# A fused attention and feed-forward kernel: single PSUM banks for the plain chunks, tile waits for new pools, and other places for the wide chunks' attention

## The chip, the core and the metric

The kernel runs on one core of a Trainium2 chip. The metric is the device time of one execution in microseconds (us). The engines are named as in the profile: PE is the matrix engine (TensorE), DVE VectorE, ACT ScalarE, POOL GpSimd, and SP the engine from whose queue nearly all transfers (DMA) are issued. PEld is PE's loading of weights.

## The reference

Inputs are `q`, `k`, `v` of shape 8 x 8 x 576 x 64 (batch, heads, sequence, head dimension), a gain `g_norm` of 64, and two weight matrices of 512 x 2048 and 2048 x 512. All is float32.

```python
kv = np.einsum('bhsd,bhse->bhde', k, v)
out = np.einsum('bhsd,bhde->bhse', q, kv)
rms = np.sqrt(np.mean(out * out, axis=-1, keepdims=True) + 1e-06)
x = (out / rms * g_norm)            # then heads are laid side by side: 4608 x 512
h = x @ w_in
g = 0.5 * h * (1.0 + erf(h / np.sqrt(2.0)))
result = g @ w_out
```

So there is a linear attention without softmax (a 64 x 64 matrix per head, then a product with the queries), a root-mean-square norm per head and token, and a two-layer network with an exact GELU.

## The kernel before

The 4608 tokens are cut into seven chunks: two **plain** chunks of 512 tokens (0 and 1) and five **wide** ones of 704, 704, 736, 736 and 704 tokens (2 to 6). Every float32 operand of a matmul is split into a rounded high part and the low rest; a product is the sum of high x high, low x high and high x low, three matmuls.

**Plain chunks** take 16 steps each. A step computes one block of 128 hidden units: `layer1` (line 621, twelve matmuls at L636 into one bank called h), `gelu` on ACT, which writes the high part `gh` and the whole value back into the bank (lines 649, 650), `rest` on DVE, which makes the low part `gl` (line 660), and `second_layer` (L668, twelve matmuls into four accumulator banks). Layer 2 of a step comes on PE behind layer 1 of the step after. Beside it run the conversion of the weights, sums of weight blocks that are stored to DRAM as `products`, and the attention of the next chunk.

**Wide chunks** (class `Fast`, lines 1096 to 1236) use a Strassen-Winograd scheme: seven products of half-size blocks in place of eight. Layer 1 has 28 steps (u = 0 to 27; group m = u // 7 and product k from `ORDER`), twelve matmuls each at L1127; layer 2 has 28 more (u = 28 to 55, list `TICKS`), at L1208. Each step reads one 512 KB block of `products` from DRAM, through a ring of six tiles (`fetch`, `used`, L547). In layer 1 the products go to pairs of banks X, Y and Z by turns, and DVE adds earlier results to them (`behind`, L564) before ACT applies GELU; the next product on the same pair waits for that. `ready` (L1186) splits an operand of layer 2: high part on ACT (L1195), low part on DVE (L1196). `combine` (L1184) adds blocks, partly on POOL.

The attention of chunk c + 1 runs inside chunk c (function `within`, line 1251) at steps that a table of numbers gives: loads of keys and queries, the key sum (`sum_keys`, L194, one pair of batches), four projections (L395) into pair W with their squares (L422, L423, L430), `fold` and `rsqrt` (the root: four small ACT copies, then nine small passes on DVE, lines 315 to 335), four `scale` (a spreading transpose on DVE, L346, into the single buffer `sq`, then a multiply on POOL, L342), four `add_blocks` (POOL, L448), and the seven `piece` splits (L456, L457). For chunk 2, called `FAST` in the table, all of this stood late (`LATE_...`: sum at step 18, projections at 20 to 26, root at 29, scales at 30 to 33, which is layer 2).

**Banks and pools.** PSUM is eight banks; before, they are four tiles of two banks each, X, Y, Z and W, for the whole kernel. A plain chunk's bank h0 or h1 is one half of X, its a0 or a1 half of W, its accumulators the halves of Y and Z. In SBUF a pool `top` gives way to `first_room` at step 13 of chunk 1 and a pool `low` to `last_room` at step 6 of chunk 2; the tiles named d are in these two rooms.

The order on each engine is the order of the program text (`manual_schedule`); a tile waits for the instructions that used it or its place before.

## Time and profile before

| what | value |
| --- | --- |
| three runs | 807.11, 813.13, 818.93 us; median 813.13 us |
| profiled execution | 813.25 us, of which the span of the profile is 811.5 us |
| PE busy | 758.6 us, 93% |
| PEld busy | 704.6 us, 87% |
| DVE busy | 540.7 us, 67% |
| ACT busy | 356.4 us, 44% |
| POOL busy | 173.8 us, 21% |
| DMA | 233.66 MB, mean 288 GB/s |

Busy shares are means over stages with different limits. The plain chunks run until 224.74 us, then come the five wide ones. The views read below are PE's waits (who released it after it stood idle), tables of busy time for stretches of the span, and the instructions of one engine in order of time; in those a number in brackets behind a row is the idle time before it, with what ended it.

### The profile page before, as it was taken

Reading aid. Unit: us, or ns where it says so; the run is one execution under the profiler, and the core shown is the slowest. Engines: PE = TensorE matmul, PEld = TensorE weight load, DVE = VectorE, ACT = ScalarE, POOL = GpSimd, SP = SyncE. Lnnn points to the kernel's source line nnn. Section 1 sums busy time; section 2 is a strip of 40 time slices with the busy share of each in tenths; the row PEclk is TensorE's granted clock in tenths of the full one; section 3 lists DMA queues with packets and bytes.
Section 4 is the critical chain, followed back from the end, with each engine's and each line's share of the span. In section 5 each row is a group of like instructions: output and inputs, shape, how many; then the busy total and the mean of one; then the engine's idle time right before and its main releaser. Section 6 shows DMA issues by size and latency. Waiting matters only on the chain.

```text
span 811.5 us, 13272 instructions
## 1 busy us (share of the span) xinstructions
PE 758.6 (93%) x5150; PEld 704.6 (87%) x5150; DVE 540.7 (67%) x720; ACT 356.4 (44%) x554; POOL 173.8 (21%) x127
## 2 busy tenths in 40 slices
PE   7799989997898996999898999899999899999997
PEld 6687777886798995999898999889998899999997
DVE  2899969989453468944659924579634679543782
ACT  3688735543352362604435415426325346123550
POOL 1000046333152107001262001380002370012000
PEclk9999999999998999999999999999999999999999
DMA  9995982794689975899688998788997788998895
GB/s 348 407 360 168 370 302 104 263 328 162 229 270 370 350 249 175 264 372 371 222 259 263 331 410 301 226 276 266 329 408 269 239 255 291 316 317 295 294 311 178
DMA packets 84962, 233.66 MB, mean 288 GB/s; under 512 B 8484, under 2 KB 29476, under 8 KB 84900
## 3 DMA queue, kind: packets, MB, share of 16 engines
q1 hardware_dynamic: 84896, 232.82, 82.0%
q8 instruction: 41, 0.67, 0.3%
q14 instruction: 21, 0.17, 0.1%
q10 hardware_dynamic: 4, 0.00, 0.0%
HBM read 193.99 MB, written 38.80 MB: 287 GB/s over the span
## 4 chain that ended last, share of the span: by engine, by line
PE 59%; DVE 21%; DMA 9%; issue 5%; ACT 4%; SPq 1%; POOL 1%; DVEq 0%; ACTq 0%
PE banks_Z L1127 8%; PE banks_Z L1208 7%; PE banks_Y L1127 7%; PE banks_X L1127 7%; PE banks_X L636 7%; PE banks_Y L1208 6%; DVE d L1196 5%; PE banks_X L1208 4%; DMA w_in<-products_in 4%; DVE d L1184 3%; PE banks_Y L668 2%; DMA w_in<-products_out 2%; DMA d<-kv_main 2%; PE banks_Z L668 2%; PE banks_W L194 2%
## 5 line engine op out<-in xcount | busy, mean ns | idle before, releaser
L1196 DVE TENSOR_TENSOR d<-d,d 128x704 fp32r<-128x704 f32 (+1 forms) x140 | 127.8, 936 | 59.4 <-ACT d L1195 59.3
L1195 ACT CAST d<-d 128x704 fp32r<-128x704 f32 (+1 forms) x140 | 104.4, 786 | 42.5 <-DVE d L1184 38.7
L1208 PE MATMUL banks_Z<-d,w_in 128*128 128x352 f32 (+1 forms) x720 | 116.8, 320 | 6.5 <-DVE d L1196 5.9
L1127 PE MATMUL banks_Z<-d,w_in 128*128 128x352 f32 (+1 forms) x684 | 116.4, 321 | 4.7 <-DVE e L564 4.7
L1208 PEld LDWEIGHTS banks_Z<-d,w_in 128*128 128x128 f32 x720 | 111.6, 191 | 9.4 <-DVE d L1196 8.6
L1127 PEld LDWEIGHTS banks_Z<-d,w_in 128*128 128x128 f32 x684 | 107.1, 191 | 7.3 <-DVE e L564 6.1
L636 PE MATMUL banks_X<-x,w_in 128*128 128x512 f32 x360 | 85.8, 389 | 13.5 <-DVE gl L660 13.5
L636 PEld LDWEIGHTS banks_X<-x,w_in 128*128 128x128 f32 x360 | 67.8, 192 | 28.5 <-DVE gl L660 18.5
L1127 PE MATMUL banks_Y<-d,w_in 128*128 128x352 f32 (+1 forms) x480 | 83.0, 324 | 6.7 <-DVE e L564 6.1
L564 DVE TENSOR_TENSOR e<-banks_Z,e 128x704 f32<-128x704 f32 (+1 forms) x53 | 47.7, 900 | 58.9 <-PE banks_Z L1127 50.6
L1184 POOL TENSOR_TENSOR d<-d,d 128x704 f32<-128x704 f32 (+1 forms) x15 | 25.7, 1715 | 283.6 <-ACT d L1139 283.6
L1127 PEld LDWEIGHTS banks_Y<-d,w_in 128*128 128x128 f32 x480 | 75.7, 193 | 10.7 <-DVE e L564 6.9
L1208 PE MATMUL banks_X<-d,w_in 128*128 128x352 f32 (+1 forms) x480 | 77.3, 318 | 6.6 <-DVE d L1196 6.6
L1127 PE MATMUL banks_X<-d,w_in 128*128 128x352 f32 (+1 forms) x480 | 81.1, 319 | 0.9 <-DMA w_in<-products_in 0.9
L1208 PEld LDWEIGHTS banks_X<-d,w_in 128*128 128x128 f32 x480 | 74.2, 191 | 7.6 <-DVE d L1196 7.6
L1127 PEld LDWEIGHTS banks_X<-d,w_in 128*128 128x128 f32 x480 | 75.1, 191 | 3.0 <-issue 2.7
L1208 PE MATMUL banks_Y<-d,w_in 128*128 128x352 f32 (+1 forms) x480 | 75.7, 316 | 1.3 <-DMA w_in<-products_out 0.7
L1208 PEld LDWEIGHTS banks_Y<-d,w_in 128*128 128x128 f32 x480 | 73.2, 189 | 2.6 <-issue 1.4
L564 DVE TENSOR_TENSOR e<-banks_Y,e 128x704 f32<-128x704 f32 (+2 forms) x31 | 27.3, 880 | 44.0 <-PE banks_Y L1208 35.2
L1184 DVE TENSOR_TENSOR d<-d,d 128x704 f32<-128x704 f32 (+1 forms) x45 | 51.0, 1133 | 0.0
L649 ACT ACTIVATE gh<-banks_X 128x512 fp32r<-128x512 f32 x32 | 19.1, 597 | 69.5 <-PE banks_X L636 64.2
L1139 ACT ACTIVATE d<-e 128x704 f32<-128x704 f32 (+1 forms) x20 | 16.0, 801 | 66.4 <-DVE e L564 66.4
(179 smaller groups left out, 1034.5 us busy)
## 6 DMA issues: line engine op xcount, KB each, us to landing
w_in<-products_in SPq DMA_DIRECT2D x140, 512.0 KB, 4.9
w_in<-products_out SPq DMA_DIRECT2D x140, 512.0 KB, 4.5
products_in<-w_in SPq DMA_DIRECT2D x40, 256.0 KB, 4.9
w_in<-w_in SPq DMA_DIRECT2D x16, 512.0 KB, 10.2
w_out<-w_out SPq DMA_DIRECT2D x16, 512.0 KB, 10.2
products_out<-w_out SPq DMA_DIRECT2D x32, 256.0 KB, 5.0
...
```

The costliest lines, as they stand in the source:

```text
L194: nc.tensor.matmul(out=ps[r, n * D:(n + 1) * D], lhsT=k[:, r], rhs=v[:, r], start=(j == 0), stop=(j == NJ),)
L564: return eng.tensor_tensor(out=out, in0=x, in1=y, op=op)
L636: nc.tensor.matmul(out=h, lhsT=parts["in", i][:, w][:, p * P:(p + 1) * P], rhs=woven(at.x[p][:, x]), start=(m + p == 0), stop=(m == 2 and ...
L649: nc.scalar.activation(out=to, in_=h, func=AF.Gelu)
L668: nc.tensor.matmul(out=ps, lhsT=x[:, ts], rhs=woven(parts["out", i][:, w]), start=(i == 0 and m == 0), stop=(m == 2 and i == NF - 1),)
L1127: nc.tensor.matmul(out=ps[:, n], lhsT=y, rhs=woven(x[:, z, kb]), start=k in (0, 2, 1) and kb + i == 0, stop=kb == 1 and i == 2, skip_group ...
L1139: nc.scalar.activation(out=self.grid(self.blocks[m][side][1])[:, half], in_=src, func=AF.Gelu)
L1184: eng.tensor_tensor(out=out, in0=x, in1=y, op=op)
L1195: nc.scalar.copy(out=t[:, 0], in_=src)
L1196: nc.vector.tensor_tensor(out=t[:, 1], in0=src, in1=t[:, 0].bitcast(F32), op=ALU.subtract)
L1208: nc.tensor.matmul(out=ps[:, a], lhsT=y, rhs=woven(x[:, z, p]), start=k in (0, 2, 1) and n + p + i == 0, stop=n == GROUPS - 1 and p == 1 a ...
```

## The change

Five things change together.

1. **Banks.** The plain chunks' banks are tiles of one bank each (h0, h1, a0, a1 and four accumulators), in two pools. The pairs X and W are made anew from the one pool before chunk 2, the pairs Y and Z from the other behind the plain chunks' last store. The projections of chunk 2 use a0 and a1, and their squares are taken in halves.
2. **Waits.** The pools `first_room`, `last_room` and the two new PSUM pools are made with `reuse_waits="tile"`: a tile waits for the users of the memory that it covers itself.
3. **Tables.** In chunk 2 the attention of chunk 3 stands in layer 1 (sum at 5, root at 16, scales at 18 to 21), and the keys are loaded at step 0. In the chunks behind it the sum stands at 1, projections at 3 to 9, the root at 13, scales at 15 to 20 and sums of blocks at 21 to 24; keys are loaded at 41 to 50 of the chunk before the one that needs them, queries at 52 and 54 of it. A reduction comes one step behind its projection.
4. **Operand passes.** `ready` is cut into `high` and `low`; in layer 1 the high part of (0, m) comes at the end of group m, the low part at the start of group m + 1, where both stood in the third step of group m + 1. `within` is called ahead of them.
5. **Places.** The rooms hold 26 d tiles (13 and 13) in place of 25 (12 and 13), the last keys of the plain kind use the tiles w_in13 and w_in14, and two pairs of places of `split_out` change sides.

```diff
-    psum = ctx.enter_context(tc.tile_pool(name="psum", bufs=1, space=PSUM))
+    acc_banks = tc.alloc_tile_pool(name="acc_banks", bufs=1, space=PSUM)
+    other_banks = tc.alloc_tile_pool(name="other_banks", bufs=1, space=PSUM)
...
-    banks = {n: psum.tile([P, 2, 512], F32, name=f"banks_{n}") for n in "XYZW"}
+    banks = {}
     def bank(name):
-        pair, n = {"h": ("X", 0), "a": ("W", 0), "acc": ("YZ", 1)}[name[:-1]], int(name[-1])
-        return banks[pair[0][n // 2 if pair[1] else 0]][:, n % 2]
+        pool = acc_banks if name.startswith("acc") else other_banks
+        return pool.tile([P, 512], F32, name=name)
...
-            nc.scalar.activation(out=self.halves(sq), in_=ps, func=AF.Square, scale=D ** -0.5)
-            nc.scalar.activation(out=self.pair_out(p), in_=ps, func=AF.Copy, scale=half_g)
+            a, b = self.halves(sq), self.pair_out(p)
+            ps = self.ps.pop(p)
+            if self.c == PLAIN:
+                parts = [(ps[half][:, :self.h], a[:, half], b[:, half]) for half in range(2)]
+            else:
+                parts = [(banks["W"][:, :, :self.h], a, b)]
+            for x, y, z in parts:
+                nc.scalar.activation(out=y, in_=x, func=AF.Square, scale=D ** -0.5)
+                nc.scalar.activation(out=z, in_=x, func=AF.Copy, scale=half_g)
...
-            first_room = tc.alloc_tile_pool(name="first_room", bufs=1, side="right")
+            first_room = tc.alloc_tile_pool(name="first_room", bufs=1, side="right", reuse_waits="tile")
...
+        def high(self, k, n):
...
-            src = self.source(k, n)
-            nc.scalar.copy(out=t[:, 0], in_=src)
+            nc.scalar.copy(out=t[:, 0], in_=self.source(k, n))
+
+        def low(self, k, n):
+            t, src = self.ops[k, n][1], self.source(k, n)
             nc.vector.tensor_tensor(out=t[:, 1], in0=src, in1=t[:, 0].bitcast(F32), op=ALU.subtract)
...
-    KEYS, QUERIES, SUM, PROJECT = (44, 47, 50, 53), (2, 5), 4, (8, 10, 12, 14)
-    NORM, SCALE, COMBINE, PIECES = (16, 17), (19, 21, 23, 25), (26, 28), range(31, 52, 3)
...
+    KEYS, QUERIES = (41, 44, 47, 50), (52, 54)
+    SUM, PROJECT, NORM = 1, (3, 5, 7, 9), (11, 13)
+    SCALE, COMBINE, PIECES = (15, 16, 18, 20), (21, 22, 23, 24), range(31, 52, 3)
+    FIRST = dict(SUM=5, PROJECT=(8, 9, 11, 12), NORM=(14, 16), SCALE=(18, 19, 20, 21), COMBINE=(22, 23, 24, 25))
+    FIRST["QUERIES"] = (0, 1)
...
+        if u - 1 in (at := FIRST["PROJECT"] if c == FAST else PROJECT):
+            nxt.reduce(at.index(u - 1), squares.pop())
+        if (p := turn("PROJECT", PROJECT)) is not None:
             nxt.project_pair(p)
-            nxt.reduce(p, nxt.square(p))
...
+            if c == FAST and not u:
+                for p in range(NP):
+                    load_kv(c + 2, p)
...
+            within(c, u)
             if (c, u) == (FAST, 6):
-                split_out(NJ2 - 1, ("w_in15", "s0"))
+                split_out(NJ2 - 1, ("w_in13", "w_in14"))
                 send()
                 low.release()
-                last_room = tc.alloc_tile_pool(name="last_room", bufs=1)
+                last_room = tc.alloc_tile_pool(name="last_room", bufs=1, reuse_waits="tile")
...
-            if n == 2 and m:
-                layer.ready(0, m - 1)
+            if n == 6 and m < GROUPS - 1:
+                layer.high(0, m)
+            if n == 0 and m:
+                layer.low(0, m - 1)
```

How the order on the engines moves is shown at three places; numbers behind names count tiles, and a row's brackets name the engine or DMA queue that it waits for. Lines are those of each kernel's own text, so one statement has two numbers.

First PE in chunk 1, from layer 1 of step 14 over layer 2 of step 13 to layer 1 of step 15. Before (L636 is layer 1, L668 layer 2):

```order
L636 MATMUL banks_X_77<-x3_374,w_in14_991 128x512
L668 MATMUL banks_Y_78<-w_out13_1044,gh_1191 128x512 [waits Activation_49]
L668 MATMUL banks_Y_78<-w_out13_1044,gh_1191 128x512
L668 MATMUL banks_Y_78<-w_out13_1044,gl_1192 128x512
...
L668 MATMUL banks_Z_79<-w_out13_1044,gh_1191 128x512 x2
L668 MATMUL banks_Z_79<-w_out13_1044,gl_1192 128x512
L636 MATMUL banks_X_77<-x0_368,w_in15_1101 128x512 [waits DVE_49]
L636 MATMUL banks_X_77<-x1_370,w_in15_1101 128x512
```

After (layer 1 is L648, layer 2 L680):

```order
L648 MATMUL h1_1279<-x3_387,w_in14_1023 128x512
L680 MATMUL acc0_483<-w_out13_1077,gh_1227 128x512 [waits Activation_49]
L680 MATMUL acc0_483<-w_out13_1077,gh_1227 128x512
L680 MATMUL acc0_483<-w_out13_1077,gl_1228 128x512 [waits DVE_49]
...
L680 MATMUL acc3_486<-w_out13_1077,gh_1227 128x512 x2
L680 MATMUL acc3_486<-w_out13_1077,gl_1228 128x512
L648 MATMUL h0_1317<-x0_381,w_in15_1135 128x512
L648 MATMUL h0_1317<-x1_383,w_in15_1135 128x512
```

The order of the blocks is the same. The wait for DVE has gone from the first matmul of layer 1 to the third of layer 2, which reads `gl`, and the two steps' layer-1 banks are two tiles, h1 and h0.

Second ACT at step 13 of chunk 1: the GELU of the step (two rows), a cast of a weight sum, and the first cast into a d tile. Before:

```order
L649 ACTIVATE gh_2094<-banks_X_77 128x512 [waits DVE_49,PE_49]
L650 ACTIVATE banks_X_77<-banks_X_77 128x512
L517 CAST w_in3_1521<-w_2042 128x2x256 [waits DMAHW4_49,DMAHW3_49]
L456 CAST d0_2103<-o_1457 128x704 [waits DMAHW5_49,DMAHW2_49,DMAHW6_49,DMAHW1_49,DMAHW7_49,DMAHW0_49,DVE_49]
L649 ACTIVATE gh_2130<-banks_X_77 128x512 [waits DVE_49,PE_49]
L650 ACTIVATE banks_X_77<-banks_X_77 128x512
L456 CAST d1_2135<-w_2058 128x704
```

After:

```order
L661 ACTIVATE gh_2166<-h0_2153 128x512 [waits PE_49,Activation_49]
L662 ACTIVATE h0_2153<-h0_2153 128x512
L529 CAST w_in3_1575<-w_2113 128x2x256 [waits DMAHW4_49,DMAHW3_49,DVE_49]
L468 CAST d0_2175<-o_1504 128x704
L661 ACTIVATE gh_2203<-h1_2190 128x512 [waits DVE_49,PE_49]
L662 ACTIVATE h1_2190<-h1_2190 128x512
L468 CAST d1_2208<-w_2129 128x704 [waits DVE_49]
```

The cast into d0 (L456 before, L468 now) no longer has the six DMA queues and DVE in its row; d1 now waits for DVE instead.

Third DVE in chunk 2, around the four spreading transposes (L346 before, L352 now). Before, where layer 2 has begun (L1196 are operand passes, L1184 a sum of blocks, the first row the last of the root):

```order
L325 SCALAR_TENSOR_TENSOR y_2896<-t_2877,y_2896 128x88 [waits DVE_49]
L1196 TENSOR_TENSOR d15_2906<-d18_2587,d15_2906 128x704 [waits DMAHW7_49,DMAHW6_49,Activation_49]
L346 STREAM_TRANSPOSE sq_2922<-y_2896 128x704 [waits DVE_49]
L1196 TENSOR_TENSOR d17_2925<-d21_2764,d17_2925 128x704 [waits DMAHW4_49,DMAHW3_49,Activation_49]
L346 STREAM_TRANSPOSE sq_2941<-y_2896 128x704 [waits Pool_49]
L1196 TENSOR_TENSOR d0_2944<-d9_2314,d0_2944 128x704 [waits Activation_49]
L346 STREAM_TRANSPOSE sq_2960<-y_2896 128x704 [waits Pool_49]
L1196 TENSOR_TENSOR d1_2963<-d12_2465,d1_2963 128x704 [waits Activation_49]
L1184 TENSOR_TENSOR d9_2314<-d9_2314,d8_2313 128x704 [waits DVE_49]
```

After, at steps 17 to 22 of layer 1 (L576 are the adds to products, L1213 an operand pass):

```order
L576 TENSOR_TENSOR e0_2797<-banks_Z_2387,e2_2734 128x704 [waits PE_49]
L576 TENSOR_TENSOR e1_2813<-banks_Y_2386,e0_2797 128x704 [waits DVE_49,PE_49]
L352 STREAM_TRANSPOSE sq_2816<-y_2774 128x704
L576 TENSOR_TENSOR banks_Z_2387<-banks_Z_2387,e2_2734 128x2x352 [waits PE_49]
L352 STREAM_TRANSPOSE sq_2835<-y_2774 128x704 [waits Pool_49]
L576 TENSOR_TENSOR banks_Y_2386<-banks_Y_2386,e3_2755 128x2x352 [waits PE_49]
L352 STREAM_TRANSPOSE sq_2853<-y_2774 128x704 [waits Pool_49]
L352 STREAM_TRANSPOSE sq_2873<-y_2774 128x704 [waits Pool_49]
L1213 TENSOR_TENSOR d17_2856<-d15_2770,d17_2856 128x704 [waits DMAHW3_49,DMAHW2_49,Activation_49]
L576 TENSOR_TENSOR e3_2890<-banks_Z_2387,e2_2871 128x704 [waits PE_49,Activation_49]
```

The transposes stood between operand passes of layer 2. They now stand between the adds of layer 1, the last two in a row, ahead of the operand pass and the add of step 22 on bank Z.

## Rows read from the trace of the kernel before

**Rows 1.** PE's waits over the span: for whom, us in total, times, longest

```profile
PE banks_X L636 <- DVE gl L660: 13.5, 12, 2.6
PE banks_X L1208 <- DVE d L1196: 6.6, 4, 2.5
PE banks_Y L1127 <- DVE e L564: 6.1, 3, 2.1
PE banks_Z L1208 <- DVE d L1196: 5.9, 6, 1.7
```

**Rows 2.** Stretches: busy us (count) of PE, PEld, DVE, ACT, POOL; clock, DMA share, GB/s

```profile
100.00:120.00 20.00, 17.42 (x149) 14.93 (x148) 14.20 (x18) 6.68 (x13) 9.04 (x8) 1.00 0.94 334
...
180.00:200.00 20.00, 16.69 (x77) 13.98 (x76) 19.66 (x25) 5.87 (x11) 6.87 (x6) 1.00 0.51 187
...
244.00:264.00 20.00, 16.65 (x90) 15.99 (x89) 6.67 (x9) 4.71 (x7) 3.58 (x3) 0.83 0.98 374
```

**Rows 3.** PE in order of time, end of chunk 1: start, duration, operation, [idle before]

```profile
207.40 2.86 PE L636 MATMUL banks_X<-x,w_in 128*128 128x512 f32 x12 [0.41 <-DVE gl L660]
...
215.15 4.49 PE L636 MATMUL banks_X<-x,w_in 128*128 128x512 f32 x12 [2.30 <-DVE gl L660]
```

**Rows 4.** Timeline of ACT, step 13 of chunk 1

```profile
212.61 0.78 ACT L456 CAST d<-o 128x704 fp32r<-128x704 f32 x1 [6.56 <-DMA products_out<-w_in]
```

**Rows 5.** Timeline of DVE, the same steps

```profile
206.66 0.68 DVE L660 TENSOR_TENSOR gl<-banks_X,gh 128x512 fp32r<-128x512 f32 x1
...
214.40 0.69 DVE L660 TENSOR_TENSOR gl<-banks_X,gh 128x512 fp32r<-128x512 f32 x1
```

**Rows 6.** Timeline of PE, chunk 2 and the start of chunk 3

```profile
224.74 1.95 PE L1127 MATMUL banks_X<-d,w_in 128*128 128x352 f32 x12
...
253.42 3.89 PE L1127 MATMUL banks_Z<-d,w_in 128*128 128x352 f32 x12 [3.35 <-DVE e L564]
257.10 3.11 PE L1127 MATMUL banks_Y<-d,w_in 128*128 128x352 f32 x12
...
308.50 2.06 PE L1208 MATMUL banks_X<-d,w_in 128*128 128x352 f32 x12 [1.02 <-DVE d L1196]
...
320.21 2.69 PE L1208 MATMUL banks_X<-d,w_in 128*128 128x352 f32 x10 [2.50 <-DVE d L1196]
...
356.08 1.95 PE L1127 MATMUL banks_X<-d,w_in 128*128 128x352 f32 x12
```

**Rows 7.** Chain that ended last, chunk 6

```profile
771.25 7.16 PE banks_X L1208 x48
```

**Rows 8.** Timeline of DVE, chunk 2

```profile
251.67 0.89 DVE L1196 TENSOR_TENSOR d<-d,d 128x704 fp32r<-128x704 f32 x1 [5.51 <-ACT d L1195]
...
306.76 0.91 DVE L346 STREAM_TRANSPOSE sq<-y 128x704 f32<-128x704 f32 x1 [1.59 <-POOL o L342]
...
311.63 2.38 DVE L1184 TENSOR_TENSOR d<-d,d 128x704 f32<-128x704 f32 x1
```

**Rows 9.** Timeline of POOL, chunk 3

```profile
403.44 1.74 POOL L342 TENSOR_TENSOR o<-o,sq 128x736 f32<-128x736 f32 x1 [4.90 <-DVE sq L346]
...
428.23 2.30 POOL L448 TENSOR_TENSOR z<-o,w 128x736 f32<-128x736 f32 x1
```

**Rows 10.** Timeline of PE, chunks 3 and 4

```profile
401.77 2.92 PE L1127 MATMUL banks_Y<-d,w_in 128*128 128x352 f32 x12 [2.07 <-DVE e L564]
...
432.13 3.55 PE L1208 MATMUL banks_Z<-d,w_in 128*128 128x352 f32 x22 [1.68 <-DVE d L1196]
...
519.08 2.14 PE L1127 MATMUL banks_Y<-d,w_in 128*128 128x368 f32 x12 [2.03 <-DVE e L564]
```

**Rows 11.** Timeline of DVE, chunk 3

```profile
397.43 1.22 DVE L315 SCALAR_TENSOR_TENSOR m<-part,t 128x92 f32<-128x92 f32 x1
...
400.66 0.25 DVE L325 SCALAR_TENSOR_TENSOR y<-t,y 128x92 f32<-128x92 f32 x1
...
404.73 0.90 DVE L564 TENSOR_TENSOR banks_Y<-banks_Y,e 128x704 f32<-128x704 f32 x1 [1.36 <-PE banks_Y L1127]
```

More of the change, by code (lines that the diff above doesn't have):

```diff
@@ L154, in load_kv @@
             main = block_tile(f"w_in{8 + p}", F32)
+        elif b == PLAIN + 2 and p > 1:
+            main = block_tile(f"w_in{11 + p}", F32)
         else:
@@ L379, in project_pair @@
         def project_pair(self, p):
-            ps = banks["W"]
+            ps = self.ps[p] = [bank(f"a{half}") if self.c == PLAIN else banks["W"][:, half] for half in range(2)]
             q = self.q.pop(p).rearrange("p (h z n) -> p h z n", h=2, z=2)
@@ L1265, in within @@
-        at = LATE_PROJECT if late else PROJECT
-        if u in at:
-            p = at.index(u)
+        if c == FAST and u in FIRST["QUERIES"]:
+            nxt.load(u)
+        if u == turn("SUM", SUM):
+            sum_keys(c + 2, banks["Z" if c == FAST else "W"][:, 0])
+        if u - 1 in (at := FIRST["PROJECT"] if c == FAST else PROJECT):
+            nxt.reduce(at.index(u - 1), squares.pop())
+        if (p := turn("PROJECT", PROJECT)) is not None:
             nxt.project_pair(p)
-            nxt.reduce(p, nxt.square(p))
@@ L1282, in within @@
-        at = LATE_PIECES if late else PIECES
-        if u in at:
-            nxt.piece(ORDER[at.index(u)])
+        if (p := turn("SCALE", SCALE)) is not None:
+            nxt.scale(p, nc.gpsimd)
+        if (n := turn("COMBINE", COMBINE)) is not None:
+            nxt.add_blocks(("T3", "T1", "T2", "T4")[n], nc.gpsimd)
+        if u in PIECES:
+            nxt.piece(ORDER[PIECES.index(u)])
+    squares = []
+    other_banks.release()
+    some_banks = tc.alloc_tile_pool(name="some_banks", bufs=1, space=PSUM, side="right", reuse_waits="tile")
@@ L1286, in linear_attn_rms_gelu_ffn @@
+    for n in "XW":
+        pair_of_banks(some_banks, n)
     for c in range(FAST, NCH):
@@ L1297, in linear_attn_rms_gelu_ffn @@
                 free += [a, b]
+                acc_banks.release()
+                more_banks = tc.alloc_tile_pool(name="more_banks", bufs=1, space=PSUM, reuse_waits="tile")
+                for name in "YZ":
+                    pair_of_banks(more_banks, name)
                 sum_out(NJ2 - 2, ("x0", "x1"))
@@ L1338, in linear_attn_rms_gelu_ffn @@
                     layer.after(k, n, (side,))
-    last_room.release()
-    first_room.release()
+    for pool in (last_room, first_room, more_banks, some_banks):
+        pool.release()
 def kernel(q, k, v, g_norm, moe_w_in, moe_w_out):
```

57 lines of the change are left out of this document (24 added, 33 removed).

## The prediction

> **What bounds the kernel now.** I read the waits of TensorE (PE) first: it is the engine that works almost all the time, so its waits are what an edit of order can win. The largest, 13.5 us, is layer 1 of the plain chunks waiting for VectorE's (DVE's) `gl` pass; then come 6.6 and 5.9 us of layer 2 waiting for operand passes (line 1196), and 6.1 us of layer 1 of the wide chunks waiting for DVE's adds [rows 1]. Next I read busy time by stretches. From 100 to 120 us PE loses 2.6 us while DVE has almost 6 us to spare, so there the wait is one of order; from 180 to 200 us DVE is busy 19.66 of 20 us, and no freedom of order makes it quicker [rows 2]. Between 244 and 264 us the granted clock is 0.83 and DMA is busy 0.98 of the time at 374 GB/s [rows 2]: two costs in one place. Then I read each place in time order. The plain chunks end with a wait of 2.30 us, after which twelve matmuls take 4.49 instead of 2.86 us [rows 3]. ScalarE (ACT) stands just before it for 6.56 us at its first cast into the new pool, for a DMA [rows 4], and the `gl` pass is late for that reason [rows 5]. Chunk 2, the first wide one, lasts from 224.74 to 356.08 us, 131.3 us [rows 6]. Its 56 steps of 1.79 us (7.16 us for four, [rows 7]) are 100.2 us; the rest is the plain chunk's tail, a key sum, projections and waits.
>
> **The change part by part. 1, banks in the plain chunks.** Before, both halves of pair X are one tile, and each step's first L636 matmul waits for the DVE pass that reads the other half. After, the wait stands at the third matmul of layer 2, one block of twelve matmuls later. A wait up to a block (2.86 us at most, [rows 3]) is covered if DVE is not itself late. All twelve waits of [rows 1] are shorter. Where DVE has room I count 3 us: the 2.6 us lost between 100 and 120 us and a little from the waits around them. Elsewhere before 207 us I count nothing, DVE being nearly full. Four pairs of ACT passes are cut into halves; they hide behind PE's blocks, and if they didn't, each would cost some tenths of a us.
>
> **2, tile waits of the room on the right.** The first cast no longer waits for six DMAs, so the wait of 2.30 us and the slow matmuls behind it (4.49 - 2.86 = 1.6 us) go. Together with part 1 this can be counted through: the `gl` pass of step 13 still ends at 206.66 + 0.68 = 207.34 us [rows 5]. By then the layer-1 block of step 14 has run. Left are layer 2 of 13, layer 1 of 15, the key sum and layer 2 of 14, four blocks of at most 2.86 us: 218.8 us at the latest, where chunk 2 began at 224.74. I take 6 us. Parts 1 and 2 give 9 us; the bounds are 3.9 us (the DMA wait alone) and 13.5 + 1.6 = 15.1 us (every wait).
>
> **3, chunk 2.** Named losses before: 3.35 us behind the cast into the second new pool [rows 8], the two products at 3.89 and 3.11 us instead of 1.95 (3.1 us more), 6.6 us of line 1208 on bank X in four waits [rows 1, 6], and ten matmuls of 2.69 us where four blocks of twelve take 7.16 (1.2 us more): 14.3 us. The four in layer 2 come from attention's multiplies and sums on GpSimd (POOL) beside DVE's passes: 2.38 us for a pass that takes 0.89 alone [rows 8]. All of that moves into layer 1. What is late next: the four spreading transposes share one buffer, so each waits for POOL's multiply of the one before (1.59 us idle in [rows 8]). In chunk 2 they stand at steps 18 to 21, the last two in a row. Counted from the end of step 18: add 0.9, transpose 0.9, multiply 1.74 [rows 9], another of POOL's passes of that size 1.74, multiply 1.74, transpose 0.9, multiply 1.74, transpose 0.9, operand pass 0.9, add of step 22 0.9: 12.3 us. PE needs that add at step 24, after five steps (8.95 us). So a new wait of 3.4 us appears. After 3.35 us the next two products lost 3.1 us; after 2.03 us in chunk 4 the product took 2.14 us and lost nothing [rows 10]; I take half, 1.5 us, and keep 0 and 3.1. The Trainium skill ("TensorE: Matmul & The Clock Gate", section on what is actually happening) says that the slow clock is the default and that activity lifts it; the granted clock of 0.83 agrees. By that rule the new wait would cost its 3.1 us in full, and the sum at the end would be 1.6 us higher. The key sum at step 5 needs four loads that are issued in step 0: 2.6 MB at 374 GB/s are 7 us, and step 5 ends some 13 us after step 0 begins; I take 0.5 us (0 to 3). Net: 14.3 - 3.4 - 1.5 - 0.5 = 8.9, taken as 9; bounds 2 (the wait with its whole clock loss, 3 us at the key sum, and half of layer 2's waits back) and 14.
>
> **4, chunks 3 to 5.** They lose 6.1 us (bank Y, three times, behind the ten small DVE passes of the root: 397.43 to 400.91 us, [rows 11]) and three times some 1.7 us, 5.1 together, on Z in layer 2 (1.68 us in chunk 3, [rows 10]; [rows 1] has 5.9 us with chunk 2's part), where POOL's sums, ending at 430.53 us [rows 9], still run 12 us after layer 2 began. Chunk 3 pays 2.92 - 1.95 = 1.0 us more for its clock. That is 12.2 us. After, the root stands at step 13 behind the last add of a group: add 0.9, root 3.5, operand pass 0.9, add 0.9 are 6.2 us against three products (5.4), so 0.8 us remain. Two transposes in a row (steps 15, 16) hold the add of step 17 by one multiply, 0.9 us more. POOL is then done about when layer 2 begins, and nothing is left there. 12.2 - 3 x 1.7 = 7.1 us; bounds 0 and 12.
>
> Does POOL slow the adds beside which it now runs? A `banks`-reading add took 0.90 us at 404.73 us [rows 11] while POOL multiplied from 403.44 to 405.18 [rows 9]; I count nothing. The Trainium skill ("SBUF — State Buffer", "Who interferes with whom") has it that only DVE instructions with two SBUF inputs contend with a reading GpSimd; layer 1's adds read PSUM and one buffer, so by it too the passes move from a place where they hurt to one where they don't. If all seven adds of three groups were slowed like line 1184, chunk 2 alone would lose 1.5 x 20 = 30 us; the 0.90 us speaks against.
>
> **5, loads.** Keys stand three steps earlier and queries at the end of layer 2 of the chunk before. Per boundary 2.6 + 1.5 MB now fall into 16 steps; weights alone take 0.52 MB per 1.79 us, 290 GB/s. The ring of six covers 10.7 us. I count 1 us of new waits over three boundaries.
>
> **Sum.** 9 + 9 + 7.1 - 1 = 24.1 us. The profiled execution took 813.25 us (span 811.5 and 1.75 around it), as good as the median of 813.13: 813.25 - 24.1 = 789 us.
>
> **Rivals.** A: DVE, not the bank, bounds the plain chunks all along. For it: 19.66 of 20 us; against it: 14.20 of 20. Then parts 1 and 2 give only 3.9 us: 794 us. B: the transposes and the slow clock behind them eat chunk 2's gain, and the chunks behind keep theirs only in part (chunk 2 gives 2, chunks 3 to 5 give 4): 813.25 - 9 - 2 - 4 + 1 = 799 us. For it: one `sq` buffer; against it: most of the 14.3 us lies elsewhere. C: DVE catches up everywhere and no new wait reaches PE (13 + 14 + 9): 777 us. D, slower: DMA. SP's one queue now holds 4.1 MB of keys and queries between two fetches of chunk 2, and again at three boundaries; at 374 GB/s each clump is 11 us. If the ring hid none, 44 us would come back: 789 + 44 = 833 us. The change is slower from the point at which over half, 24 us, is not hidden. For it: DMA at 0.98 in 244 to 264; against it: the same loads stood in that stretch and PE waited there for ACT and DVE, not for a fetch.
>
> **How the numbers follow.** 789 us has 0.42 (its own range 783 to 795), A 0.18, B 0.17, C 0.18, D 0.05. The range of 776 to 802 us takes in A, B and most of C. About 2%, 16.3 us, is what a measurement here can tell from no change. Below 797 us lie the forecast, A, C and a little of B: 0.81; within 2% most of B: 0.14; slower 0.05.
>
> **What would show it.** Right: no wait of layer 1 for `gl` in the plain chunks but some of layer 2; no DMA wait of the first cast; chunk 2 begins near 219 and ends near 342 us; in it one wait of 3 to 4 us on bank Z behind a transpose; two waits below 1 us per chunk behind it; none on Z in layer 2. Wrong: fetches (`w_in` from `products`) as releasers of PE for several us, DVE busy all through the plain chunks with the same end, or layer-1 adds above 1.5 us.

## The result

The changed kernel takes 764.74 us (median of four runs, 762.89 to 765.42), where the kernel before takes 814.61 us (four runs, 807.11 to 818.93): a ratio of 0.9393, with a 95% interval of 0.932 to 0.9467. The gain is about 50 us; 24 were forecast, and 764.74 us lies below the range of 776 to 802 us. The profiled execution took 765.12 us, of which the span is 763.0; before, the span was 811.5, so 48.5 us are to be found.

First the stretches of the changed kernel, cut where the stages begin (the key of the columns is that of [rows 2]): the plain chunks' steps from their first layer-2 matmul, layer 1 and layer 2 of chunk 2, and chunks 3 to 5.

```profile
29.18:204.51 175.33, 171.96 (x992) 145.03 (x989) 164.10 (x253) 105.41 (x194) 45.56 (x41) 1.00 0.81 292
204.51:276.12 71.61, 64.63 (x477) 60.77 (x476) 38.17 (x49) 30.40 (x47) 30.04 (x23) 0.93 0.84 303
276.12:326.29 50.17, 50.17 (x338) 50.12 (x337) 39.08 (x48) 24.37 (x35) 2.48 (x2) 1.00 0.95 339
326.29:658.18 331.89, 330.90 (x2403) 321.64 (x2402) 218.78 (x267) 146.73 (x210) 75.38 (x42) 1.00 0.89 313
```

The same four stages of the kernel before:

```profile
36.68:224.74 188.06, 174.57 (x992) 145.74 (x989) 160.00 (x248) 102.45 (x182) 46.04 (x41) 0.99 0.72 257
224.74:292.49 67.75, 63.46 (x478) 59.77 (x476) 31.59 (x36) 28.03 (x42) 18.12 (x16) 0.95 0.90 321
292.49:356.08 63.59, 55.39 (x338) 52.47 (x337) 51.62 (x60) 27.01 (x41) 17.71 (x8) 0.95 0.76 249
356.08:706.65 350.57, 336.18 (x2402) 323.17 (x2401) 223.99 (x267) 147.28 (x210) 79.60 (x42) 1.00 0.86 299
```

Subtract row from row. The start, before the first layer-2 matmul, is 36.68 - 29.18 = 7.5 us shorter; the plain steps 188.06 - 175.33 = 12.7; layer 1 of chunk 2 is 3.9 us longer, its layer 2 13.4 shorter (9.6 together); chunks 3 to 5 are 18.7 us shorter. Together that is 48.5 us, the whole of it.

| stage | forecast gain, us | measured, us |
| --- | --- | --- |
| plain chunks, the start with them (terms 1 and 2) | 9 | 20.2 |
| chunk 2 (term 3) | 9 | 9.6 |
| chunks 3 to 5 (terms 4 and 5) | 6.1 | 18.7 |

PE's waits over the whole span of the changed kernel, in the columns of [rows 1], which they answer to:

```profile
PE banks_Z L1139 <- DVE d L1213: 3.7, 1, 3.7
PE banks_Z L1139 <- DVE e L576: 3.3, 3, 2.6
PE acc L680 <- DVE gl L672: 3.2, 7, 0.9
```

Where twelve waits for `gl` cost 13.5 us, seven at the accumulators now cost 3.2. The waits of layer 2 (L1225) for operand passes, 12.5 us before, are gone. Two longer waits on bank Z are left, both in chunk 2. PE in order of time there, which answers to [rows 6]:

```profile
204.51 1.95 PE L1139 MATMUL banks_X<-d,w_in 128*128 128x352 f32 x12
...
227.98 3.86 PE L1139 MATMUL banks_Z<-d,w_in 128*128 128x352 f32 x12 [3.68 <-DVE d L1213]
231.77 1.45 PE L401 MATMUL banks_W<-d,kv 64*64 64x224 f32 x12
233.15 2.48 PE L1139 MATMUL banks_X<-d,w_in 128*128 128x352 f32 x12
...
267.18 2.96 PE L1139 MATMUL banks_Z<-d,w_in 128*128 128x352 f32 x12 [2.61 <-DVE e L576]
269.93 2.77 PE L1139 MATMUL banks_Y<-d,w_in 128*128 128x352 f32 x12
```

Chunk 2 begins at 204.51 us, not at 219. The wait at 267.18 is the one forecast for step 24, with 2.61 us in place of 3.4. The wait at 227.98, at step 8, was not forecast. What stands behind each, and which edit carries which gain, the experiments tell.

### The profile page after: what moved, and what is told of

Its sections match the earlier page's. It is cut to its first block, busy times and chain, and to the rows that moved or that the text cites. A ratio compares the mean times of both kernels' runs of the same rounds, so it can differ in the third digit from the quotient of the medians.

```text
span 763.0 us, 13264 instructions
## 1 busy us (share of the span) xinstructions
PE 743.9 (97%) x5150; PEld 698.7 (92%) x5150; DVE 533.6 (70%) x720; ACT 356.5 (47%) x562; POOL 165.8 (22%) x127
## 4 chain that ended last, share of the span: by engine, by line
PE 62%; DVE 4%; POOL 2%; issue 1%; ACT 1%; ACTq 0%; DVEq 0%; POOLq 0%
PE banks_Z L1225 14%; PE banks_Z L1139 12%; PE banks_Y L1225 10%; PE banks_X L1225 9%; PE banks_Y L1139 8%; PE banks_X L1139 7%; PE banks_W L401 2%; DVE e L576 1%; POOL o L348 1%; PE banks_W L200 1%; DVE d L1213 1%; DVE sq L352 1%; ACT d L1151 0%; ACT d L1209 0%; DVE t L331 0%
## 5 line engine op out<-in xcount | busy, mean ns | idle before, releaser
L1213 DVE TENSOR_TENSOR d<-d,d 128x704 fp32r<-128x704 f32 (+1 forms) x140 | 136.9, 1000 | 32.8 <-ACT d L1209 32.6
L1139 PE MATMUL banks_Z<-d,w_in 128*128 128x352 f32 (+1 forms) x684 | 117.6, 323 | 7.2 <-DVE d L1213 3.7
L1209 ACT CAST d<-d 128x704 fp32r<-128x704 f32 (+1 forms) x140 | 104.5, 787 | 19.8 <-DVE d L1196 19.7
L1225 PE MATMUL banks_Z<-d,w_in 128*128 128x352 f32 (+1 forms) x720 | 112.9, 315 | 0.1
L1225 PEld LDWEIGHTS banks_Z<-d,w_in 128*128 128x128 f32 x720 | 110.0, 189 | 0.4 <-DVE d L1213 0.4
L576 DVE TENSOR_TENSOR e<-banks_Z,e 128x704 f32<-128x704 f32 (+1 forms) x53 | 47.6, 899 | 67.9 <-PE banks_Z L1139 51.1
L1196 POOL TENSOR_TENSOR d<-d,d 128x704 f32<-128x704 f32 (+1 forms) x15 | 25.7, 1715 | 314.5 <-ACT d L1151 314.5
L648 PE MATMUL h<-x,w_in 128*128 128x512 f32 x360 | 82.9, 380 | 0.0
L1139 PE MATMUL banks_Y<-d,w_in 128*128 128x352 f32 (+1 forms) x480 | 81.1, 319 | 0.0
L1139 PE MATMUL banks_X<-d,w_in 128*128 128x352 f32 (+1 forms) x480 | 80.4, 317 | 0.2 <-ACT e L1160 0.2
L648 PEld LDWEIGHTS h<-x,w_in 128*128 128x128 f32 x360 | 67.8, 189 | 10.1 <-issue 0.6
L680 PE MATMUL acc<-w_out,gh 128*128 128x512 f32 x256 | 76.8, 381 | 0.0
L1225 PE MATMUL banks_Y<-d,w_in 128*128 128x352 f32 (+1 forms) x480 | 74.8, 315 | 0.6 <-DVE e L576 0.6
L1225 PE MATMUL banks_X<-d,w_in 128*128 128x352 f32 (+1 forms) x480 | 75.3, 315 | 0.0
L1225 PEld LDWEIGHTS banks_Y<-d,w_in 128*128 128x128 f32 x480 | 73.2, 189 | 0.9 <-DVE e L576 0.9
L1225 PEld LDWEIGHTS banks_X<-d,w_in 128*128 128x128 f32 x480 | 73.4, 189 | 0.0
L576 DVE TENSOR_TENSOR e<-banks_Y,e 128x704 f32<-128x704 f32 (+2 forms) x31 | 27.2, 879 | 50.7 <-PE banks_Y L1225 35.5
L680 PEld LDWEIGHTS acc<-w_out,gh 128*128 128x128 f32 x256 | 47.9, 189 | 7.7 <-issue 1.4
L680 PE MATMUL acc<-w_out,gl 128*128 128x512 f32 x128 | 49.5, 386 | 3.4 <-DVE gl L672 3.2
```

What stands on the lines that cost most here:

```text
L576: return eng.tensor_tensor(out=out, in0=x, in1=y, op=op)
L648: nc.tensor.matmul(out=h, lhsT=parts["in", i][:, w][:, p * P:(p + 1) * P], rhs=woven(at.x[p][:, x]), start=(m + p == 0), stop=(m == 2 and ...
L680: nc.tensor.matmul(out=ps, lhsT=x[:, ts], rhs=woven(parts["out", i][:, w]), start=(i == 0 and m == 0), stop=(m == 2 and i == NF - 1),)
L1139: nc.tensor.matmul(out=ps[:, n], lhsT=y, rhs=woven(x[:, z, kb]), start=k in (0, 2, 1) and kb + i == 0, stop=kb == 1 and i == 2, skip_group ...
L1196: eng.tensor_tensor(out=out, in0=x, in1=y, op=op)
L1209: nc.scalar.copy(out=t[:, 0], in_=self.source(k, n))
```

## The experiments

Each is the changed kernel with one edit, so its own time is set against 764.74 us and its stages against the rows above. All ratios are against runs of the kernel before on the same chip. The medians of the kernel before in these sets are 811.0 to 814.6 us, so a difference of some 3 us between two runs of different sets is no larger than that, and rests on the stages of the profiles.

**The banks of the plain chunks as pairs again.** The key in the diff is the one of before; nothing else moves.

```diff
+    plain = {n: (acc_banks if n in "YZ" else other_banks).tile([P, 2, 512], F32, name=f"plain_{n}") for n in "XYZW"}
     def bank(name):
-        pool = acc_banks if name.startswith("acc") else other_banks
-        return pool.tile([P, 512], F32, name=name)
+        pair, n = {"h": ("X", 0), "a": ("W", 0), "acc": ("YZ", 1)}[name[:-1]], int(name[-1])
+        return plain[pair[0][n // 2 if pair[1] else 0]][:, n % 2]
```

> The changed kernel, but the banks of the plain chunks are halves of four tiles of two banks again (the rest of the change stays). Theory 1 (single banks free the start as well as the steps): the first 40 us lose the 7.5 us that they gained and the steps of the plain chunks some 8 to 11 us, so chunk 2 begins near 222 us and the time is 780 to 784 us. Theory 2 (the gain of the plain chunks comes from the tile waits of the first room, single banks are worth 3 us as forecast): chunk 2 begins near 208 us, 768 us. In both, chunks 2 to 6 last as long as in the changed kernel, 558.5 us.

Measured: 780.68 us (four runs, 774.21 to 782.32), ratio 0.96 (0.955 to 0.965). Chunk 2 begins at 222.56 us, 18.05 us later; what follows lasts 557.9 us, as in the changed kernel. This is theory 1. The start and the steps:

```profile
0.00:38.74 38.74, 30.81 (x279) 25.15 (x279) 20.07 (x47) 15.70 (x31) 2.19 (x15) 0.82 0.97 375
38.74:222.56 183.82, 172.67 (x993) 144.66 (x990) 158.69 (x246) 103.31 (x190) 46.03 (x41) 1.00 0.72 259
```

and its largest wait, of the whole span and then of the start:

```profile
PE plain_X L649 <- DVE gl L673: 11.0, 10, 2.6
...
PE plain_X L639 <- DVE gl L669: 1.9, 1, 1.9
```

The start is 9.6 us longer than in the changed kernel (38.74 against 29.18), the steps 8.5. In the start PE is idle for 7.9 us in small waits, where the changed kernel has 3.6 us; this is 4.3 of the 9.6 us. The other 5.3 us are longer matmuls (30.81 against 25.55 us) at a granted clock of 0.82. With the tile waits still in place the steps are 188.06 - 183.82 = 4.2 us shorter than in the kernel before. The waits of layer 1 for `gl` in the steps are those of the kernel before, but for one of 0.16 us and the last, of 2.30 us [rows 3], which is gone with the slow matmuls behind it:

```profile
214.70 2.75 PE L649 MATMUL plain_X<-x,w_in 128*128 128x512 f32 x12
```

So this is what the tile waits are worth beside pairs, near the lower bound of the forecast, 3.9 us.

**Only the two layer-1 banks as one tile.**

```diff
+    plain = {n: (acc_banks if n in "YZ" else other_banks).tile([P, 2, 512], F32, name=f"plain_{n}") for n in "X"}
     def bank(name):
+        pair, n = {"h": ("X", 0), "a": ("W", 0), "acc": ("YZ", 1)}[name[:-1]], int(name[-1])
+        pair = pair[0][n // 2 if pair[1] else 0]
+        if pair in plain:
+            return plain[pair][:, n % 2]
```

> The changed kernel with only the two layer-1 banks of the plain chunks (h0, h1) as halves of one tile again; accumulators and attention banks stay single. All pairs together cost 18 us of chunk 2's begin (222.56 against 204.51). Theory 1 (the layer-1 bank carries nearly all of the steps, 11.0 us of waits for gl and the 1.9 us of the second step, and the slow clock behind these; the others only the start's attention): chunk 2 begins at 217 to 219 us, 777 to 780 us in all. Theory 2 (the start's attention and accumulator banks carry half): chunk 2 begins at 212 to 214 us, 772 to 774 us.

Measured: 778.3 us (774.07 to 780.08), ratio 0.957 (0.9521 to 0.9619). Chunk 2 begins at 217.70 us, so theory 1: h0 and h1 carry 13.2 of the 18 us in the profiled executions (by the medians 13.6 of 15.9). Of these 2.8 us lie in the start (31.93 against 29.18) and 10.4 in the steps (185.77 against 175.33). The 4.9 us left can't be put down to the other banks alone: the start of this run has a granted clock of 1.00 where that with all pairs has 0.82, and the fastest runs of the two agree (774.07 and 774.21 us). The steps' waits are back:

```profile
PE plain_X L653 <- DVE gl L677: 9.9, 8, 2.6
```

**Both rooms without tile waits.**

```diff
-            first_room = tc.alloc_tile_pool(name="first_room", bufs=1, side="right", reuse_waits="tile")
+            first_room = tc.alloc_tile_pool(name="first_room", bufs=1, side="right")
...
-                last_room = tc.alloc_tile_pool(name="last_room", bufs=1, reuse_waits="tile")
+                last_room = tc.alloc_tile_pool(name="last_room", bufs=1)
```

> The changed kernel without tile waits in the two rooms (first_room and last_room wait for their whole predecessors again). Theory 1 (tile waits are worth the one stall at the first cast, 2.3 us and the slow clock of 1.6 us behind it, and with single banks the stall is partly covered): chunk 2 begins 2 to 4 us later than 204.5 us, and the second room costs up to 3 us in chunk 2: 767 to 772 us. Theory 2 (the forecast's 6 us): chunk 2 begins near 210.5 us, 771 us and above. Rival: by now nothing waits there, 765 us.

Measured: 762.95 us (762.5 to 764.88), ratio 0.9413 (0.9387 to 0.9439): the rival, nothing waits there any more. And yet the stall itself is back, and longer than in [rows 4]. ACT in order of time, with the first cast into the room:

```profile
198.58 0.78 ACT L468 CAST d<-o 128x704 fp32r<-128x704 f32 x1 [9.69 <-DMA products_out<-w_in]
199.27 0.59 ACT L661 ACTIVATE gh<-h 128x512 fp32r<-128x512 f32 x1
```

In the changed kernel ACT runs this cast at 189.59 us without a wait:

```profile
189.59 0.78 ACT L468 CAST d<-o 128x704 fp32r<-128x704 f32 x1
193.59 0.60 ACT L661 ACTIVATE gh<-h 128x512 fp32r<-128x512 f32 x1 [3.22 <-PE h L648]
```

ACT stands for 9.69 us and the GELU behind it is late, but chunk 2 begins at 203.72 us, no later than with tile waits. PE is busy for 171.85 of the 175.22 us of the plain steps, as with them: a late GELU no longer stops the next block of layer 1, which has a bank of its own. Beside pairs the tile waits gave 4.2 us, beside single banks they give nothing: both edits hide the same stall [rows 3]. This run also names the wait at step 8 otherwise than the changed kernel's profile does:

```profile
227.22 3.50 PE L1139 MATMUL banks_Z<-d,w_in 128*128 128x352 f32 x12 [3.06 <-DMA w_in<-products_in]
```

A fetch, then, where the other profile named a DVE pass that ended in the same moment. The next run asks for it.

**The second query load of chunk 3 at step 4 of chunk 2.**

```diff
-    FIRST["QUERIES"] = (0, 1)
+    FIRST["QUERIES"] = (0, 4)
...
-            nxt.load(u)
+            nxt.load(FIRST["QUERIES"].index(u))
```

> The changed kernel with the second load of chunk 3's queries (0.7 MB) at step 4 of chunk 2 in place of step 1, behind two fetches in place of ahead of them. Theory 1 (the new wait of 3.7 us before step 8 is for a fetch that stands behind keys, stores and queries in SP's one queue): the wait shrinks by the time of such a load, 1.7 us at 410 GB/s or more, and the slow matmuls behind it by part of 3 us: 760 to 763 us. Theory 2 (the wait is for the DVE pass that the profile names): nothing changes there, 764 to 765 us.

Measured: 761.56 us (760.99 to 762.46), ratio 0.9392 (0.9368 to 0.9416), theory 1. PE's two waits of the stretch that follow from transfers:

```profile
226.51 2.03 PE L1139 MATMUL banks_Z<-d,w_in 128*128 128x352 f32 x12 [2.49 <-DMA w_in<-products_in]
...
234.52 2.06 PE L1139 MATMUL banks_Y<-d,w_in 128*128 128x352 f32 x12 [0.50 <-DMA w_in<-products_in]
```

The wait is 1.2 us shorter, and its matmuls take 2.03 us in place of 3.86: the granted clock of chunk 2 stays at 1.00, and the chunk takes 117.54 us in place of 121.78. The ratio is that of the changed kernel, so the gain of 3 us rests on these rows and on times that do not overlap. In the changed kernel SP's queue shows why the fetch is late. The rows are issues on SP, here stores of the plain chunk's result, the query load and the two fetches of steps 8 and 9:

```profile
213.81 2.49 SPq L689 DMA_DIRECT2D out<-d  x4
217.09 0.34 SPq L381 DMA_DIRECT2D d<-q  x1
217.53 2.72 SPq L559 DMA_DIRECT2D w_in<-products_in  x2
```

The ring's place was free when step 2 ended, at 212.6 us; its fetch went out at 217.53.

**Queue order alone**: the query load at step 3 and the four stores at step 5, no engine's work moved.

```diff
-            nxt.load(u)
+            nxt.load(u, u == 1)
+        if (c, u) == (FAST, 3):
+            nc.sync.dma_start(out=nxt.late_q, in_=wide_q[nxt.c - PLAIN][1])
...
-                store(acc.pop(c - 1), (c - 1) * CH, [x[:, z * DM:(z + 1) * DM] for x in (s, t) for z in range(2)])
+                late_out = [x[:, z * DM:(z + 1) * DM] for x in (s, t) for z in range(2)]
+                for x, ps in zip(late_out, acc.pop(c - 1)):
+                    nc.scalar.copy(out=x, in_=ps)
...
+            if (c, u) == (FAST, 5):
+                for n, x in enumerate(late_out):
+                    nc.sync.dma_start(out=out[(c - 1) * CH + n * P:(c - 1) * CH + (n + 1) * P, :], in_=x)
```

> The changed kernel with two groups of transfers further back in SP's queue in chunk 2, no instruction of another engine moved: the second query load of chunk 3 at step 3 (before: 1) and the four stores of the plain chunk's result at step 5 (before: 1), so that the fetches of steps 8 and 9 go out ahead of them. Theory 1 (the wait before step 8 is SP's queue order): the wait of 3.1 to 3.7 us falls under 1 us, with it most of the slow clock in the same place: 758 to 761 us. Theory 2 (bandwidth: the same bytes must pass before): a fetch wait of 2 us or more stays, at this step or the next ones, 762 to 765 us.

Measured: 768.74 us (767.54 to 769.05), ratio 0.9468 (0.9432 to 0.9505), some 4 us slower than the changed kernel (chunk 2 takes 1.8 us more, 123.61); neither theory. The fetch wait did fall, to 0.9 us, but step 6 casts into the tile that the stores read from, and ACT waits for them, with PE behind it. ACT, then PE:

```profile
232.36 0.78 ACT L1212 CAST d<-d 128x704 fp32r<-128x704 f32 x1 [7.21 <-DMA out<-d]
```

```profile
233.84 3.76 PE L1142 MATMUL banks_X<-d,w_in 128*128 128x352 f32 x12 [7.11 <-ACT e L1163]
```

The order of the queue was the cause of the fetch's delay, and this is what was late next: a store put behind fetches holds its source tile longer.

**Two buffers for the spread root.**

```diff
-            bc = work.tile([P, WIDEST], F32, name="sq")[:, :sizes[self.c]]
+            if self.c > PLAIN and n % 2:
+                bc = work.tile([P, WIDEST], I32, name="z", bufs=2).bitcast(F32)[:, :sizes[self.c]]
+            else:
+                bc = work.tile([P, WIDEST], F32, name="sq")[:, :sizes[self.c]]
```

> The changed kernel, in the wide chunks with two buffers for the spread root (sq and, for every second pair, a z tile that is free then). Theory 1 (the wait of 2.6 us at step 24 of chunk 2 comes from transposes that wait for POOL's multiply in one buffer): that wait goes, and the 2.1 us lost by the slow clock behind it: 760 us. Rival (POOL's seven passes in a row are the chain, so that the add of step 22 is as late with two buffers): 764 to 765 us and the wait stays above 2 us.

Measured: 757.54 us (756.79 to 757.9), ratio 0.934 (0.9317 to 0.9364), theory 1 and 2.5 us better than it: the wait at step 24 is gone, and chunks 3 to 5 are 2.1 us shorter too (329.80 against 331.89 us). DVE in the changed kernel, the last two transposes and what stands behind them:

```profile
261.94 0.91 DVE L352 STREAM_TRANSPOSE sq<-y 128x704 f32<-128x704 f32 x1 [1.58 <-POOL o L348]
264.64 0.91 DVE L352 STREAM_TRANSPOSE sq<-y 128x704 f32<-128x704 f32 x1 [1.79 <-POOL o L348]
265.47 0.85 DVE L1213 TENSOR_TENSOR d<-d,d 128x704 fp32r<-128x704 f32 x1
266.25 0.88 DVE L576 TENSOR_TENSOR e<-banks_Z,e 128x704 f32<-128x704 f32 x1
```

and with two buffers:

```profile
258.73 0.90 DVE L355 STREAM_TRANSPOSE sq<-y 128x704 f32<-128x704 f32 x1
259.56 0.87 DVE L355 STREAM_TRANSPOSE z<-y 128x704 f32<-128x704 f32 x1
260.35 1.51 DVE L1216 TENSOR_TENSOR d<-d,d 128x704 fp32r<-128x704 f32 x1
261.79 0.88 DVE L579 TENSOR_TENSOR e<-banks_Z,e 128x704 f32<-128x704 f32 x1
```

The add of step 22 ends at 262.7 us in place of 267.1, and PE needs it for step 24 at 263.1 us. Chunk 2 is 5.8 us shorter: 4.4 are this wait with its slow matmuls, and 1.3 are fewer slow matmuls behind the wait at step 8, which is as long as in the changed kernel (3.75 us) and which this edit does not touch.

**Chunk 2's attention late again.**

```diff
-    FIRST = dict(SUM=5, PROJECT=(8, 9, 11, 12), NORM=(14, 16), SCALE=(18, 19, 20, 21), COMBINE=(22, 23, 24, 25))
+    FIRST = dict(SUM=5, PROJECT=(20, 22, 24, 26), NORM=(28, 29), SCALE=(30, 31, 32, 33), COMBINE=(34, 35, 36, 37))
...
-        if u in PIECES:
-            nxt.piece(ORDER[PIECES.index(u)])
+        pieces = (39, 41, 43, 46, 49, 52, 54) if c == FAST else PIECES
+        if u in pieces:
+            nxt.piece(ORDER[pieces.index(u)])
```

> The changed kernel, but in chunk 2 the projections stand at steps 20 to 26, the root at 28 and 29, the scales at 30 to 33 and the sums of blocks at 34 to 37 (as before), pieces from 39 on; the key sum, loads, banks and chunks 3 to 6 stay changed. Theory 1 (the forecast's trade: layer 1 pays for the attention, layer 2 gets back more): layer 1 of chunk 2 is shorter by 2.6 us of wait at step 24 and its slow clock, layer 2 longer by 10 to 13 us: 770 to 774 us. Theory 2 (layer 2 was slow for another reason, the second room's and the loads' places): layer 2 of chunk 2 stays below 54 us, 763 to 766 us.

Measured: 773.92 us (772.11 to 774.27), ratio 0.953 (0.9493 to 0.9567), theory 1. Chunk 2 takes 130.3 us where it took 121.8. Layer 2 alone is 63.27 us, as before the change (63.59), and its waits are those of [rows 1] again:

```profile
PE banks_X L1225 <- DVE d L1213: 6.5, 4, 2.5
```

**Chunks 3 to 5 with the attention at the steps of before.**

```diff
-    SUM, PROJECT, NORM = 1, (3, 5, 7, 9), (11, 13)
-    SCALE, COMBINE, PIECES = (15, 16, 18, 20), (21, 22, 23, 24), range(31, 52, 3)
+    SUM, PROJECT, NORM = 4, (8, 10, 12, 14), (16, 17)
+    SCALE, COMBINE, PIECES = (19, 21, 23, 25), (26, 27, 28, 29), range(31, 52, 3)
```

> The changed kernel, but in chunks 3 to 5 the key sum, projections, root, scales and sums of blocks stand at the steps of before (sum 4, projections 8 to 14, root 17, scales 19 to 25, sums of blocks 26 to 29); loads, operand passes and chunk 2 stay changed. Theory 1 (the 18.7 us that chunks 3 to 5 gained come from these places): a wait of some 2 us on bank Y behind the root and one of 1.5 us on Z in layer 2 come back in each, with slow clock once: 776 to 783 us. Theory 2 (they come from the earlier loads and the operand passes): under 769 us and no wait on Y.

Measured: 776.31 us (775.19 to 776.97), ratio 0.9556 (0.9508 to 0.9604). The three chunks take 343.49 us, 11.6 more than in the changed kernel, with these waits among others:

```profile
PE banks_Z L1225 <- DVE d L1213: 3.7, 5, 1.3
PE banks_Z L1139 <- DMA w_in<-products_in: 2.8, 3, 1.1
PE banks_Y L1139 <- DVE e L576: 1.7, 3, 0.6
```

Theory 1 by the time, but not by all its waits. The wait behind the root costs 0.6 us in each chunk here and cost 2 us before [rows 1]; the operand passes and the reductions keep their new places in this run, and which of them does it was not tried. And the 2.8 us in the second row are for fetches, of which the kernel before had 1.2 us in these chunks on all banks together: the old places beside the new loads cost something that the kernel before did not pay.

**The operand passes at their old place.**

```diff
-            if n == 6 and m < GROUPS - 1:
-                layer.high(0, m)
-            if n == 0 and m:
-                layer.low(0, m - 1)
+            if n == 2 and m:
+                layer.ready(0, m - 1)
```

> The changed kernel with both passes of the operand (0, m) in the third step of the next group again, behind the attention's work of that step. Theory 1 (the places of the attention carry the gain, the passes are hidden either way): 763 to 766 us. Theory 2 (an operand pass right behind the root or a transpose holds the adds of layer 1): new waits on Y or Z of 0.5 to 1 us in each of chunks 2 to 5, 767 to 771 us.

Measured: 767.96 us (765.76 to 768.59), ratio 0.9446 (0.9404 to 0.9487): theory 2, by a little. Chunks 3 to 5 take 336.18 us, 4.3 more than in the changed kernel, of them 3.4 in new waits:

```profile
PE banks_Z L1139 <- DVE e L576: 4.1, 7, 1.1
```

(0.7 us in the same chunks of the changed kernel.) By the medians of all runs the difference is 3.2 us, and the intervals of the ratios overlap; the two profiled executions differ by 0.6 us alone, since chunk 2 is 3.3 us shorter in this one (118.47 us).

**A better version.** Two causes were found in chunk 2, so they were mended together, by edits shown above. A version with the queries at step 5 and the stores at step 8 does not compute the reference's function, and its 756.34 us are not used. Then came the two buffers with the queue order of the fifth run.

> The same queue order and two buffers for the spread root in the wide chunks. Theory 1 (two causes that add): no wait of chunk 2 above 1 us, no slow clock in it, 751 to 754 us. Theory 2 (the bandwidth moves the wait on): 755 to 758 us, as with the two buffers alone.

Measured: 761.32 us (six runs, 760.55 to 762.3), ratio 0.9378 (0.9347 to 0.941): neither theory, for the wait on ACT behind the stores is in it as well, with 7.0 us. Last, the two buffers with the query load at step 4, the stores where they were:

> The changed kernel with the second query load of chunk 3 at step 4 of chunk 2 (stores at step 1 as they are) and two buffers for the spread root in the wide chunks. Theory 1 (two causes that add: 3.2 us and 7.2 us below the changed kernel's 764.7 when each was taken alone): 753 to 755 us, the only waits of chunk 2 above 1 us are one or two for fetches, 3.5 us together. Theory 2 (an earlier end of the transposes changes nothing once the fetches are late again): 757 to 759 us.

Measured: 755.36 us (six runs, 754.27 to 757.53), ratio 0.9295 (0.9252 to 0.9338), just above the range of theory 1. The two gains alone were 3.2 and 7.2 us, 10.4 together; the run has 9.4. Chunk 2 takes 113.06 us, 8.7 less than in the changed kernel, at a granted clock of 1.00, with two fetch waits in it:

```profile
PE banks_Z L1142 <- DMA w_in<-products_in: 1.2, 1, 1.2
...
PE banks_Y L1142 <- DMA w_in<-products_in: 1.0, 1, 1.0
```

Its slowest run is 5 us below the fastest of the changed kernel, though the two were not timed in one set of runs.

## Why the prediction was right or wrong

**Terms 1 and 2, 9 us together, measured 20.2: this is the step that failed first.** It failed in three ways. One is the sentence "Elsewhere before 207 us I count nothing, DVE being nearly full". DVE was busy 160.00 of the 188.06 us of the plain steps before; the stretch of 19.66 of 20 us in [rows 2] was no bound of the stage. After, it does 164.10 us of work in 175.33, and between 120 and 140 us both engines are full:

```profile
120.00:140.00 20.00, 20.00 (x110) 16.51 (x109) 19.79 (x29) 12.03 (x25) 10.36 (x11) 1.00 0.65 232
```

A full stretch does not say what an engine could do in the whole stage if it might start earlier. The plain steps got 12.7 of the 15.1 us that I had named as the most. Another is the start: I worked the part out from stretches behind 100 us and gave the start no row at all, though it shows what pairs cost. The start of the kernel before, then of the changed one:

```profile
0.00:36.68 36.68, 28.33 (x279) 23.27 (x279) 19.23 (x45) 15.73 (x31) 2.20 (x15) 0.91 0.97 374
...
0.00:29.18 29.18, 25.55 (x278) 20.99 (x279) 16.49 (x41) 14.00 (x27) 2.19 (x15) 1.00 0.96 364
```

PE stood idle for 8.35 us there, now for 3.63, and its matmuls took 28.33 us at a granted clock of 0.91, now 25.55 at 1.00: 4.7 + 2.8 = 7.5 us came back, half as much as my bound for all the rest. The third is the split: 3 us for the banks and 6 for the tile waits. By the runs it is 18 us in the profile for the banks (16 by the medians, of which some 6 seem to hang on the slow clock: the one run with pairs at a mean clock of 0.998 took 774.21 us) and, beside single banks, nothing that can be measured for the tile waits of the rooms. The Trainium skill ("PSUM — Partial Sum Buffer", "PSUM bank collisions raise a hardware error") has as its rule to guard PSUM by bank, or finer, and not by address; a tile of two banks guards more than the rule asks. What the coarser guard costs here the run with only h0 and h1 in one tile shows: 13.6 us.

**Term 3, 9 us, measured 9.6, and 8.5 by the run that undoes it.** The net is right, its parts are not, and two errors cancel by luck. Named losses of 14.3 us were too few: layer 2 of chunk 2 alone gave back 13.4 us, 8.2 of idle PE (63.59 - 55.39) and 5.2 of matmuls longer than now (55.39 - 50.17), where I had found 6.6 + 1.2. One row that I missed are two blocks of twelve, at a granted clock of 0.72; elsewhere in this stage two take 3.74 us:

```profile
324.79 5.27 PE L1208 MATMUL banks_Z<-d,w_in 128*128 128x352 f32 x24 [0.51 <-DVE d L1196]
```

The cause that I gave for the four waits holds: of nine sums of blocks on DVE (line 1184) four took 2.35 to 2.38 us beside POOL and five 0.88 to 0.89; now they take 0.885 in the mean. On the other side stands the wait at step 8, 3.68 us and 3.1 us of slow matmuls behind it (3.86 + 1.45 + 2.48 against 1.95 + 0.82 + 1.95), which I had not seen. The wait at step 24 is right in place and in mechanism: one `sq` buffer, transposes that wait for POOL, 2.61 us and 1.8 us of slow matmuls against 3.4 and 1.5. The key sum, for which I allowed 0.5 us, didn't wait.

**Term 4, 7.1 us, and term 5, -1 us, measured 18.7.** The mechanism was right and its size was off on both sides. The losses of before in chunks 3 to 5 were 350.57 - 336.18 = 14.4 us of idle PE and 5.3 us of matmuls that were longer than now (336.18 - 330.90): 19.7 us, of which I had named 12.2, the three or four largest rows. And the new waits of 1.7 us per chunk came to 0.7 us in all. The chain behind the root, which I had at 6.2 us against 5.4, is shorter. DVE in chunk 3, the last add ahead of the root, the root's first and last pass, the operand pass and the add that PE waits for:

```profile
358.19 0.90 DVE L576 TENSOR_TENSOR banks_Y<-banks_Y,e 128x704 f32<-128x704 f32 x1 [0.89 <-PE banks_Y L1139]
358.99 0.25 DVE L321 SCALAR_TENSOR_TENSOR m<-part,t 128x92 f32<-128x92 f32 x1
...
361.25 0.25 DVE L331 SCALAR_TENSOR_TENSOR y<-t,y 128x92 f32<-128x92 f32 x1
361.42 0.88 DVE L1213 TENSOR_TENSOR d<-d,d 128x704 fp32r<-128x704 f32 x1
362.22 0.88 DVE L576 TENSOR_TENSOR e<-banks_Z,e 128x704 f32<-128x704 f32 x1
```

The root's nine passes (not ten) take 2.5 us, not the 3.5 between the first and last row of [rows 11], whose first pass alone took 1.22 us; the same pass is 0.25 us here. So the add ends at 363.10 us, and PE needs it at 363.36. Undone alone, the places of the attention cost 11.6 us in these chunks, 2.8 of them in new waits for fetches, and the operand passes 4.3, to which I had given no term. These are not shares of the 18.7 us, and what the earlier loads bring by themselves was not tried. Term 5 did not come: the changed kernel has no wait for a fetch in these chunks, where I had expected 1 us more.

The adds beside POOL, for which I counted nothing, kept 0.88 to 0.90 us in layer 1 of chunk 2. The operand passes, which read two SBUF tiles, took 1.81 us (at 248.59 us) and 1.90 us (at 275.16) beside it, where I had 0.9. That only such passes contend, as I put it, no run here shows.

**The rivals.** A (DVE bounds the plain chunks) falls by the row of 20.00 and 19.79 us. B falls: transposes cost chunk 2 only 4.4 us. C (DVE catches up everywhere) was nearest, and its mechanism held in the plain chunks and in chunks 3 to 5, but its sum of 36 us was still built on the same short list of losses, and 777 us is 12 us too long. D (transfers) is true on a small scale: one clump in SP's queue cost 6.8 us at one place, and none at the three boundaries behind.
